# Small tiles moved to one constant tile, the global tokens' block moved to last but one, and the last store cut in parts

## The chip, the cores and the metric

The kernel runs on one core of a Trainium2 chip, in one launch. The metric is device time in microseconds (us), lower is better. Matrix products run on the tensor engine (PE, with PEld for the loads of its stationary operand). The vector engine (DVE), the scalar engine (ACT) and GpSimd (POOL) do the rest, and SyncE (SP) issues all DMAs, in one queue.

## What is computed

Eight batches of eight heads of attention with 32 global tokens and 512 local ones, and behind it a gated layer without a non-linearity:

```python
s_g = scale * q_g @ k_all.T          # 32 global queries see all 544 keys
s_l = scale * q_l @ [k_g, k_l].T     # 512 local queries: the global keys, and local ones within 32 positions
out_g, out_l = sm(s_g) @ v_all, sm(s_l) @ v_all
x = concat(out_g, out_l)             # (8 * 544, 512): all heads of a token side by side
a, b = x @ w1, x @ w2                # 512 -> 1024
return ((a * b) @ w3) @ w_out        # 1024 -> 1024 -> 512
```

## The kernel before, in words

Precision: a matrix product of two float32 operands is made of three products of the fast type fp32r. Each operand is split in a high part (a copy rounded to fp32r, `hi_of`) and a low part (what is left, `lo_of`), and high by high, low by high and high by low are summed in PSUM.

Attention: for each head `scores` (L528; L521 for the first 16 heads) makes the band of local scores in four windows, `minus_max` (L532, DVE) adds the mask and finds the maxima (tile `mn`, four numbers a row), `exps` (L536, ACT) makes the exponentials and their sums (`sm`), transposes (L565) turn them, and `values` (L641, L646) multiplies by v. The global queries of two heads go together: `g_scores` (L696, L688), maxima `mg`, sums `smg`. Tile `G` of `values` takes some of its columns through DRAM: `move_out` writes `gd`, `move_in` (L598) reads it back, both by SP's queue.

The layer: w3 and w_out are folded into one matrix at the start (`fold`, L934; result `w34`, high and low part). The tokens then pass in 17 blocks: 16 of 256 local tokens (two to a batch) and one of the 256 global tokens of all batches. A block has four quarters. In a quarter `first` makes two 128-row tiles of a and two of b: for each, over four pairs of heads p, three matmuls of 256 columns,

```python
nc.tensor.matmul(d, wh[:, k, c, :], x[:, 0, 0:w], ...)   # L797
nc.tensor.matmul(d, wh[:, k, c, :], x[:, 1, 0:w], ...)   # L798
nc.tensor.matmul(d, wl[:, k, c, :], x[:, 0, 0:w], ...)   # L799
```

so that a part of w1 and w2 (tiles `w12h`, `w12l`) is the stationary operand and the tokens (`x`) are the moving one. `gate_a` (ACT) and `gate_b` (DVE) multiply a by b, `gh` and `gl` are the two parts of that product, and `second` (L827 to L829) multiplies it by w34: the stationary operand is 128 columns of `gh` or `gl`, the moving one 512 columns of `w34`. After the fourth quarter `evict` (L834) copies the two accumulators of a block to SBUF (`o`) and `store` (L842; L844 for the global block) writes them to DRAM. Block 16, the last, is the global one (`quarter`: `key, w = (divmod(k, 2), 256) if k < 2 * B else ((B, 0), TG)`).

Order: every step is put on a list with the engines that may run it, an assumed duration, what it waits for, and a due time out of the table `DUE`. `list_schedule` plays the engines forward with the assumed durations and gives the free engine the ready step that is due first. The outcome is the order in each engine's queue. At run time every engine takes its queue strictly in that order.

Memory: tiles of a pool lie one behind the other in SBUF in the order in which their tags first appear, each rounded up to a multiple of 32 bytes. The pools follow each other: `const`, `p1`, `p2`, `w12a`, and then `early` and in its place `w12b`.

Of the kernel before, what the change touches and what calls it, by code (L numbers as in the profile page):

```python
# [30 lines left out]
def i(ap):  # L31
# [285 lines left out]
def band_attention_glu_kernel(  # L317
# [527 lines left out]

    def unpack(step, raw, dst):
# [606 lines left out]
```

## Time and profile before

| | |
|---|---|
| time, median of 3 runs | 877.1 us (876.62 to 877.37) |
| the profiled execution | 877.64 us, of which the span from first to last instruction is 875.9 us |
| TensorE clock granted | 0.995 of full speed over the span |
| PE busy | 849.7 us (97%) |
| DVE, ACT, POOL busy | 561.0, 538.3, 404.5 us |
| DMA | 109.75 MB, 125 GB/s mean |

The span is what the profile shows engine by engine, and the time has 1.7 us more around it. Matmuls are pipelined: the duration that the profile gives for one is longer than the distance from its start to the next one's start, and it is that distance, called pitch here, that adds up to the span.

### The profile page before, as it was taken

To read this page: it belongs to the slowest core of one execution; us is meant where nothing else is said; L and a number is where in the kernel's file an instruction comes from. 1 tells how busy PE (TensorE), PEld (TensorE's weight loads), DVE (VectorE), ACT (ScalarE), POOL (GpSimd) and SP (SyncE) were. 2 spreads that over 40 slices of the span, in tenths; PEclk is the share of its full clock that TensorE was granted. 3 is DMA by queue.
4 is the path that set the end of the run, shared out by engine and by line. 5 is a ranking of instruction groups with operands and counts; after the bars stand their busy time and mean duration, and the time that the engine had idled before them with its cause. 6 is when DMAs were issued, how large, how long until landed. Compare 5 with 4: busy or idle time off the path is not lost.

```text
span 875.9 us, 17696 instructions
## 1 busy us (share of the span) xinstructions
PE 849.7 (97%) x5794; PEld 766.2 (87%) x5794; DVE 561.0 (64%) x1464; ACT 538.3 (61%) x1450; POOL 404.5 (46%) x505
## 2 busy tenths in 40 slices
PE   4999999999999999999999999999999999999995
PEld 3666579899999999999999999999999999999994
DVE  3778777756777776779677777676757677421111
ACT  3666777756677777767676767776857677312111
POOL 1022445654665556656465656566666545200000
PEclk9999999999999999999999999999999999999998
DMA  8686655554746464655455645655555534100000
GB/s 280 201 264 219 198 158 139 159 118 93 160 94 171 100 149 97 146 132 147 100 132 130 155 105 124 144 128 135 127 137 123 128 95 96 27 25 1 25 25 25
DMA packets 194228, 109.75 MB, mean 125 GB/s; under 512 B 150040, under 2 KB 158232, under 8 KB 194136
## 3 DMA queue, kind: packets, MB, share of 16 engines
q1 hardware_dynamic: 194136, 108.61, 48.5%
q8 instruction: 46, 0.75, 0.4%
q14 instruction: 46, 0.38, 0.2%
HBM read 85.52 MB, written 20.28 MB: 121 GB/s over the span
## 4 chain that ended last, share of the span: by engine, by line
PE 92%; DMA 2%; POOL 1%; issue 1%; SPq 1%; DVE 1%; ACT 1%; POOLq 0%; DVEq 0%; ACTq 0%
PE bp L797 7%; PE ap L797 7%; PE bp L798 7%; PE bp L799 7%; PE ap L799 7%; PE ap L798 7%; PE acc L827 7%; PE acc L829 7%; PE acc L828 7%; PE av L646 7%; PE w L934 6%; PE s L528 5%; PE s L521 3%; PE t L565 3%; PE av L641 3%; PE sg L696 1%
## 5 line engine op out<-in xcount | busy, mean ns | idle before, releaser
L797 PE MATMUL ap<-x,w12h 128*128 128x256 f32 x544 | 156.6, 288 | 0.0
L797 PE MATMUL bp<-x,w12h 128*128 128x256 f32 x544 | 156.1, 287 | 0.0
L799 PE MATMUL ap<-x,w12l 128*128 128x256 f32 x544 | 154.3, 284 | 0.0
L798 PE MATMUL ap<-x,w12h 128*128 128x256 f32 x544 | 154.2, 283 | 0.0
L798 PE MATMUL bp<-x,w12h 128*128 128x256 f32 x544 | 154.1, 283 | 0.0
L799 PE MATMUL bp<-x,w12l 128*128 128x256 f32 x544 | 154.0, 283 | 0.0
L536 ACT ACTIVATE P<-P,mn 128x192 f32<-128x192 f32 (+1 forms) x256 | 121.3, 475 | 16.9 <-DVE mn L532 16.7
L797 PEld LDWEIGHTS ap<-x,w12h 128*128 128x128 f32 x544 | 104.0, 191 | 2.2 <-issue 0.4
L798 PEld LDWEIGHTS ap<-x,w12h 128*128 128x128 f32 x544 | 104.3, 192 | 1.6
L797 PEld LDWEIGHTS bp<-x,w12h 128*128 128x128 f32 x544 | 104.1, 191 | 1.7 <-issue 0.2
L798 PEld LDWEIGHTS bp<-x,w12h 128*128 128x128 f32 x544 | 104.2, 191 | 1.5
L799 PEld LDWEIGHTS ap<-x,w12l 128*128 128x128 f32 x544 | 104.2, 192 | 0.0
L799 PEld LDWEIGHTS bp<-x,w12l 128*128 128x128 f32 x544 | 104.1, 191 | 0.0
L532 DVE CUSTOM_DVE_ANT_0 P<-s,cs 128x192 f32<-128x192 f32 (+1 forms) x256 | 87.0, 385 | 26.4 <-PE s L528 18.0
L452 POOL TENSOR_TENSOR kl<-kr,kh 128x608 fp32r<-128x608 f32 x42 | 63.7, 1516 | 38.3 <-ACT kh L449 30.6
L660 DVE TENSOR_TENSOR u<-av,cb 64x352 f32<-64x352 f32 x112 | 57.5, 518 | 36.6 <-ACT cb L449 34.9
L449 ACT COPY cb<-av 64x352 f32<-64x352 f32 x94 | 41.9, 446 | 40.1 <-PE av L646 38.7
L646 PE MATMUL av<-PT,vs 128*128 128x192 f32 x448 | 64.4, 271 | 0.0
L646 PEld LDWEIGHTS av<-PT,vs 128*128 128x128 f32 x448 | 60.2, 190 | 0.8
L934 PE MATMUL w<-wo,w3f 128*128 128x512 f32 x128 | 60.1, 605 | 0.0
L452 POOL TENSOR_TENSOR TT<-TT 128x352 fp32r<-128x352 f32 x35 | 34.8, 993 | 44.9 <-ACT TT L449 39.8
L452 POOL TENSOR_TENSOR qs<-qr,qs 64x512 fp32r<-64x512 f32 x34 | 45.1, 1326 | 20.9 <-ACT qs L449 15.8
(807 smaller groups left out, 2148.7 us busy)
## 6 DMA issues: line engine op xcount, KB each, us to landing
kr<-in_kd_t_dram SPq DMA_DIRECT2D x96, 152.0 KB, 3.0
raw_w<-in_w_t_dram SPq DMA_DIRECT2D x24, 512.0 KB, 4.9
kpr<-in_kp_t_dram SPq DMA_DIRECT2D x32, 272.0 KB, 3.4
out_dram<-o SPq DMA_DIRECT2D x34, 256.0 KB, 2.9
R<-rd SPq DMA_DIRECT2D x64, 128.0 KB, 3.2
gd<-TT SPq DMA_DIRECT2D x112, 64.0 KB, 2.6
vr<-in_v_t_dram SPq DMA_DIRECT2D x28, 256.0 KB, 3.0
G<-gd SPq DMA_DIRECT2D x112, 64.0 KB, 2.7
```

Of the source, the lines that this page charges most:

```text
L452: (eng or nc.gpsimd).tensor_sub(dst, src, f(hi))
L532: nc.vector.tensor_tensor_reduce(blk(n, e), T["st", n][:, e, 0 : WIN[e][1]], masks[e], -0.125, 3.0e38, ALU.add, ALU.min, T["mn", n][:, e : ...
L536: nc.scalar.activation(blk(n, e), blk(n, e), AF.Exp, bias=T["mn", n][:, e : e + 1], scale=-1.0, accum_out=T["sm", n // 2][:, n % 2, e : e ...
L646: nc.tensor.matmul(av[:, o : o + 32 * (s1 - s0)], v, PT[:, s0:s1, y, j], start=False, stop=(j % 2 == 1 and (plain or y == 1)), skip_group_ ...
L660: nc.vector.tensor_add(T["u", n // 2][r : r + 64, x], T.pop(("av", n, x))[r : r + 64, 0:352], T["cb", n][r : r + 64, x])
L797: nc.tensor.matmul(d, wh[:, k, c, :], x[:, 0, 0:w], start=(k == m % 2 == 0), stop=False, skip_group_check=True)
L798: nc.tensor.matmul(d, wh[:, k, c, :], x[:, 1, 0:w], start=False, stop=False, skip_group_check=True)
L799: nc.tensor.matmul(d, wl[:, k, c, :], x[:, 0, 0:w], start=False, stop=(k == 3), skip_group_check=True)
L827: nc.tensor.matmul(a, gh[:, m % 2, sl], wh, start=(m == 0), stop=False)
L828: nc.tensor.matmul(a, gh[:, m % 2, sl], wl, start=False, stop=False)
L829: nc.tensor.matmul(a, gl[:, m % 2, sl], wh, start=False, stop=(m == 7))
L934: nc.tensor.matmul(T["w34", t], T["w3f", t, j // 4][:, j % 4], T["wo"][:, j], start=(j == 0), stop=(j == 7))
```

## The change

A tile `small` of 64 bytes is allocated in `const`, and `mn`, `mg` and `smg`, until now tiles of 32 bytes each in `p2` (two of `mn`) and `p1`, become slices of it. It stands in front of `w34`, whose tiles are allocated later. So the start of many tiles shifts by 64 bytes. In the built programs they begin at these addresses modulo 128:

| tiles | used as | before | now |
|---|---|---|---|
| w12h, w12l | stationary in `first` | 64 | 0 |
| x | moving in `first` | 64 | 64 |
| gh, gl | stationary in `second` | 64 | 64 |
| w34 | moving in `second` | 0 | 64 |
| QG | stationary in `g_scores` | 0 | 64 |
| kph, kpl (and their second halves) | moving in `g_scores` | 64 (0) | 64 (0) |
| vgs | stationary, L641 | 0 | 0 |
| vs | stationary, L646 | 64 | 64 |
| G, PT | moving, L641 and L646 | 0 | 64 |
| qs; kh, kl | stationary; moving in L528 | 64; 64 | 64; 64 |

The global block becomes block 15 and the second half of the last batch block 16. In the last quarter of block 16 the second product of one 128-token tile is made in two halves of 256 columns, each copied and stored by itself. The other tile stays whole. The numbers of `DUE` are all replaced, with a few more of them, since there are more steps. The code lines are one to three lower or higher in the new program (L797 is L798 there, L827 is L830, L834 is L837, L842 is L845).

```diff
 DUE = tuple(int(x) / 100 for x in """
-    -655 -3767 4986 -976 9590 1663 3525 1681 -604 7022 298 5732 -137 5816 154 5532 -86 5558 180 5514 -1205 5768 -3363 1416
+    1514 -13720 -3729 -9726 1511 -1470 2180 -5679 -837 8859 -6169 8856 2561 8285 -7174 8072 2818 8049 7770 7400 -1214 8643 6068 3083
...
+    small = const.tile([128, 16], F32, tag="small", name="small")
...
-        T["mn", n] = p2.tile([128, 4], F32, tag="mn", name=f"mn{n}")
+        T["mn", n] = small[:, 4 * (n % 2) : 4 * (n % 2) + 4]
...
-            T["mg", m // 2] = p1.tile([128, 1], F32, tag="mg", name=f"mg{m}")
+            T["mg", m // 2] = small[:, 8:9]
...
-        T["smg", g] = p1.tile([128, 1], F32, tag="smg", name=f"smg{g}")
+        T["smg", g] = small[:, 9:10]
...
-        for t in range(0, w, 128) if ts is None else ts:
+        c = slice(0, 512) if ts is None or len(ts) == 1 else slice(256 * ts[1], 256 * ts[1] + 256)
+        for t in range(0, w, 128) if ts is None else ts[:1]:
...
-        key, w = (divmod(k, 2), 256) if k < 2 * B else ((B, 0), TG)
+        key, w = (((B, 0), TG) if k == 2 * B - 1 else (divmod(min(k, 2 * B - 1), 2), 256))
...
-        split = k % 2 == 0 and q == 0
+        split = key[1] == 0 and q == 0
...
-        parts = [(e,) for e in range(0, w, 128)] if last else [None]
+        parts = [(0,), (128, 0), (128, 1)] if last else [None]
...
+            for e, h in [(0, None), (128, 0), (128, 1)] if last else [(e, None) for e in range(0, w, 128)]:
...
-        add(("xh", B, p, 0), only("ACT", COST["xh"]), base(NH) + 34, g, split_x, (B, p, 0), 0, xg[:, p], TG, 0)
-        add(("xl", B, p, 0), either("xl"), base(NH) + 35, [("xh", B, p, 0)],
+        add(("xh", B, p, 0), only("ACT", COST["xh"]), base(NH) + 8, g, split_x, (B, p, 0), 0, xg[:, p], TG, 0)
+        add(("xl", B, p, 0), either("xl"), base(NH) + 9, [("xh", B, p, 0)],
```

The built order shows the shift at three places. First SP's queue at the start of the program, before: `kq` holds the keys and `qp` the queries of the first two heads, `kpr` the keys for the global queries, `cs` identity and mask, `raw_w`, `raw_w12s` and `raw_wo` weights.

```order
L394 DMA qp_97<-in_q_t_dram 128x512
L424 DMA kpr_99<-in_kp_t_dram 128x544
L430 DMA QG_95<-in_qg_t_dram 64x4x32 x2
L370 DMA cs<-in_cst_dram 128x576
L898 DMA raw_w12s_0_108<-in_w_t_dram 128x512
L898 DMA raw_w_0_110<-in_w_t_dram 128x1024
L898 DMA raw_w12s_1_114<-in_w_t_dram 128x512
L400 DMA kq_116<-in_kd_t_dram 128x608
L424 DMA kpr_118<-in_kp_t_dram 128x544
L898 DMA raw_wo_0_120<-in_wo_t_dram 128x1024
```

The same place now:

```order
L425 DMA kpr_98<-in_kp_t_dram 128x544
L896 DMA raw_w_0_100<-in_w_t_dram 128x1024
L431 DMA QG_96<-in_qg_t_dram 64x4x32 x2
L401 DMA kq_106<-in_kd_t_dram 128x608
L395 DMA qp_110<-in_q_t_dram 128x512
L371 DMA cs<-in_cst_dram 128x576
L896 DMA raw_w12s_1_113<-in_w_t_dram 128x512
L896 DMA raw_w12s_0_117<-in_w_t_dram 128x512
L896 DMA raw_w12s_2_119<-in_w_t_dram 128x512
L425 DMA kpr_121<-in_kp_t_dram 128x544
L896 DMA raw_wo_0_123<-in_wo_t_dram 128x1024
```

`kq` has moved from eighth place to fourth (QG's row counts once), in front of `cs` and of all of `raw_w12s`. The weights `raw_w` have moved up to second place, in front of QG.

Second the end of PE's queue, before: the last quarter of the global block, `second` for its last two rows of `w34`.

```order
L827 MATMUL acc_0_128_11066<-w34h_937,gh__11188 128x512
L828 MATMUL acc_0_128_11066<-w34l_938,gh__11188 128x512
L829 MATMUL acc_0_128_11066<-w34h_937,gl__11196 128x512
L827 MATMUL acc_0_0_11065<-w34h_937,gh__11188 128x512
L828 MATMUL acc_0_0_11065<-w34l_938,gh__11188 128x512
L829 MATMUL acc_0_0_11065<-w34h_937,gl__11196 128x512
L827 MATMUL acc_0_0_11065<-w34h_1000,gh__11188 128x512
L828 MATMUL acc_0_0_11065<-w34l_1001,gh__11188 128x512
L829 MATMUL acc_0_0_11065<-w34h_1000,gl__11196 128x512
L827 MATMUL acc_0_128_11066<-w34h_1000,gh__11188 128x512
L828 MATMUL acc_0_128_11066<-w34l_1001,gh__11188 128x512
L829 MATMUL acc_0_128_11066<-w34h_1000,gl__11196 128x512
```

The same place now, the second half of the last batch. Ahead of these rows stand six more of 256 columns like the first six.

```order
L830 MATMUL acc_1_128_10971<-w34h_935,gh__11093 128x256
L831 MATMUL acc_1_128_10971<-w34l_936,gh__11093 128x256
L832 MATMUL acc_1_128_10971<-w34h_935,gl__11101 128x256
L830 MATMUL acc_1_128_10971<-w34h_963,gh__11093 128x256
L831 MATMUL acc_1_128_10971<-w34l_964,gh__11093 128x256
L832 MATMUL acc_1_128_10971<-w34h_963,gl__11101 128x256
L830 MATMUL acc_1_0_10970<-w34h_935,gh__11093 128x512
L831 MATMUL acc_1_0_10970<-w34l_936,gh__11093 128x512
L832 MATMUL acc_1_0_10970<-w34h_935,gl__11101 128x512
L830 MATMUL acc_1_0_10970<-w34h_963,gh__11093 128x512
L831 MATMUL acc_1_0_10970<-w34l_964,gh__11093 128x512
L832 MATMUL acc_1_0_10970<-w34h_963,gl__11101 128x512
```

The tile that is cut in halves is finished first, and the whole tile, 512 columns wide, ends the queue.

Third the last rows of SP's queue, before: four stores of local tokens and the two of the global block.

```order
L842 DMA out_dram<-o_0_128_10753 128x512
L842 DMA out_dram<-o_0_0_10755 128x512
L842 DMA out_dram<-o_1_0_11041 128x512
L842 DMA out_dram<-o_1_128_11043 128x512
L844 DMA out_dram<-o_0_0_11210 4x32x512
L844 DMA out_dram<-o_0_128_11212 4x32x512
```

The same place now:

```order
L845 DMA out_dram<-o_0_0_None 128x512
L845 DMA out_dram<-o_0_128_None 128x512
L847 DMA out_dram<-o_0_0_None 4x32x512
L847 DMA out_dram<-o_0_128_None 4x32x512
L845 DMA out_dram<-o_1_128_0_11112 128x256
L845 DMA out_dram<-o_1_128_1_11121 128x256
L845 DMA out_dram<-o_1_0_None 128x512
```

The two global stores (4x32x512) stand one block earlier, and the queue ends with two half stores and a whole one of local tokens.

## Rows read from the trace of the kernel before

**Rows 1.** The page: span, and busy time of each engine.

```profile
span 875.9 us, 17696 instructions
PE 849.7 (97%) x5794; PEld 766.2 (87%) x5794; DVE 561.0 (64%) x1464; ACT 538.3 (61%) x1450; POOL 404.5 (46%) x505
```

**Rows 2.** Waits of PE over the span: for what, total us, times, longest.

```profile
PE sg L688 <- DMA QG<-in_qg_t_dram: 5.2, 1, 5.2
PE s L521 <- DMA kq<-in_kd_t_dram: 4.9, 1, 4.9
PE av L641 <- DMA G<-gd: 2.2, 2, 1.2
PE s L521 <- DVE mg L715: 1.2, 1, 1.2
```

**Rows 3.** Timeline of PE in block 16: start us, duration us, instruction.

```profile
857.45 0.28 PE L797 MATMUL bp<-x,w12h 128*128 128x256 f32 x1
...
860.20 0.28 PE L799 MATMUL bp<-x,w12l 128*128 128x256 f32 x1
860.32 0.40 PE L827 MATMUL acc<-w34h,gh__11164 128*128 128x512 f32 x1
...
863.12 0.39 PE L827 MATMUL acc<-w34h,gh__11188 128*128 128x512 f32 x1
```

**Rows 4.** Windows: busy us of each engine, then PEclk, DMA share, GB/s.

```profile
800.00:840.00 40.00, 40.00 (x285) 37.50 (x284) 6.92 (x10) 6.49 (x11) 0.00 (x0) 1.00 0.04 15
840.00:866.00 26.00, 26.00 (x167) 23.24 (x165) 5.44 (x8) 4.76 (x8) 0.00 (x0) 1.00 0.06 21
```

**Rows 5.** The page's groups: line, operation, count | busy us, mean ns.

```profile
L797 PE MATMUL ap<-x,w12h 128*128 128x256 f32 x544 | 156.6, 288 | 0.0
L799 PE MATMUL bp<-x,w12l 128*128 128x256 f32 x544 | 154.0, 283 | 0.0
```

**Rows 6.** Timeline of SP at the end: start us, us, engine, operation.

```profile
865.42 1.29 ACT L834 COPY o<-acc 128x512 f32<-128x512 f32 x2 [3.56 <-PE acc L829]
865.69 0.40 PE L829 MATMUL acc<-w34h,gl__11196 128*128 128x512 f32 x1
866.03 1.40 SPq L844 DMA_DIRECT2D out_dram<-o  x2
```

**Rows 7.** Waits of SP's queue, 860 to 877 us: for what, us, times, longest.

```profile
SPq L1454 <- DMA out_dram<-o: 7.4, 1, 7.4
```

**Rows 8.** Windows in the last store and in a local block's stores, columns as above.

```profile
870.00:872.00 2.00, 0.00 (x0) 0.00 (x0) 0.00 (x0) 0.00 (x0) 0.00 (x0) 0.63 0.26 101
810.80:811.80 1.00, 1.00 (x11) 1.00 (x10) 0.95 (x2) 0.00 (x0) 0.00 (x0) 1.00 1.01 385
```

**Rows 9.** DMA issues, 809 to 816 us: count, KB each, median us to landing.

```profile
out_dram<-o SPq DMA_DIRECT2D x2, 256.0 KB, 2.1
```

**Rows 10.** The chain that ended last, in the first 25 us: start, us, what.

```profile
5.09 6.97 DMA kq<-in_kd_t_dram
12.06 0.14 issue
12.20 3.33 PE s L521 x8
...
16.94 2.18 PE sg L688 x4
19.12 1.66 PE w L934 x2
```

**Rows 11.** Windows at the start, columns as above.

```profile
3.00:12.10 9.10, 2.15 (x4) 1.18 (x4) 3.10 (x8) 1.56 (x3) 1.57 (x4) 1.00 0.92 290
25.00:30.00 5.00, 5.00 (x22) 3.64 (x21) 3.64 (x13) 3.11 (x12) 0.00 (x0) 1.00 0.62 179
```

**Rows 12.** L696's first kph matmul at 186 us: duration ns min/median/max.

```profile
L696 PE MATMUL sg<-kph,QG x1: 284/284/284, 186.0 to 186.0; 128*128 128x272 f32 x1
```

**Rows 13.** L696's next two matmuls, at 186.1 and 186.2 us.

```profile
L696 PE MATMUL sg<-kph,QG x1: 288/288/288, 186.1 to 186.1; 128*128 128x272 f32 x1
L696 PE MATMUL sg<-kpl,QG x1: 288/288/288, 186.2 to 186.2; 128*128 128x272 f32 x1
```

**Rows 14.** Groups of PE by form, 200 to 760 us: busy us, mean ns.

```profile
L641 PE MATMUL av<-G,vgs 128*128 128x256 f32 x50 | 14.4, 287 | 0.0
```

More of the change, by code (lines that the diff above doesn't have):

```diff
@@ L823, in second, with evict, store @@
         gh, gl = T["gh", m // 2 % 2], T["gl", m // 2 % 2]
-        for t in range(0, w, 128) if ts is None else ts:
+        c = slice(0, 512) if ts is None or len(ts) == 1 else slice(256 * ts[1], 256 * ts[1] + 256)
+        for t in range(0, w, 128) if ts is None else ts[:1]:
             sl = slice(t, t + tw)
-            a = T["acc", key, t][0:tw]
-            nc.tensor.matmul(a, gh[:, m % 2, sl], wh, start=(m == 0), stop=False)
-            nc.tensor.matmul(a, gh[:, m % 2, sl], wl, start=False, stop=False)
-            nc.tensor.matmul(a, gl[:, m % 2, sl], wh, start=False, stop=(m == 7))
-    def evict(key, w, t, eng=None):
-        tw = min(w, 128)
-        o = p2.tile([128, 512], F32, tag="o", name=f"o{key[0]}_{key[1]}_{t}", bufs=NO)
-        (nc.scalar.copy if eng is nc.scalar else nc.vector.tensor_copy)(o[0:tw], T.pop(("acc", key, t))[0:tw])
-        T["o", key, t] = o
-    def store(key, w, t):
-        tw = min(w, 128)
-        o = T.pop(("o", key, t))
+            a = T["acc", key, t][0:tw, c]
+            part = dict(skip_group_check=m > 5)
+            nc.tensor.matmul(a, gh[:, m % 2, sl], wh[:, c], start=(m == 0), stop=False, **part)
+            nc.tensor.matmul(a, gh[:, m % 2, sl], wl[:, c], start=False, stop=False, **part)
+            nc.tensor.matmul(a, gl[:, m % 2, sl], wh[:, c], start=False, stop=(m in (5, 7)), **part)
+    def evict(key, w, t, cols=None, eng=None):
+        tw, c = min(w, 128), slice(0, 512) if cols is None else slice(256 * cols, 256 * cols + 256)
+        o = p2.tile([128, 512], F32, tag="o", name=f"o{key[0]}_{key[1]}_{t}_{cols}", bufs=NO)
+        (nc.scalar.copy if eng is nc.scalar else nc.vector.tensor_copy)(o[0:tw, c], T["acc", key, t][0:tw, c])
+        T["o", key, t, cols] = o
+    def store(key, w, t, cols=None):
+        tw, c = min(w, 128), slice(0, 512) if cols is None else slice(256 * cols, 256 * cols + 256)
+        o = T.pop(("o", key, t, cols))
         if key[0] < B:
             r = key[0] * S + 32 + 256 * key[1] + t
-            nc.sync.dma_start(out[r : r + 128], o)
+            nc.sync.dma_start(out[r : r + 128, c], o[:, c])
         else:
@@ L1291, in quarter @@
                         take("acc", 2, ("acc", k, e), me)
-                add(me, only("PE", COST["second"] * c / len(parts)), u + 1.1 * j + (ts[0] / 64 if ts else 0), deps, second, key, w, m + j, ts)
+                add(me, only("PE", COST["second"] * c / (2 * len(ts) if ts else 1)), u + 1.1 * j + (sum(ts) / 64 if ts else 0), deps, second, key, w, m + j, ts)
                 read(me, ("gh", n), ("gl", n), *[("acc", k, e) for e in range(0, w, 128)])
         if q == 3:
-            for e in range(0, w, 128):
-                me = ("out", k, e)
-                take("o", NO, ("o", k, e), me)
-                add(me, dict(ACT=(COST["out"], False, 0), DVE=(691, False, HOLD_A)), u + 2.5, [("second", k, 7, (e,) if last else None)],
-                    evict, key, w, e, eng=True)
+            for e, h in [(0, None), (128, 0), (128, 1)] if last else [(e, None) for e in range(0, w, 128)]:
+                me = ("out", k, e, h)
+                take("o", NO, ("o", k, e, h), me)
+                ns = (COST["out"], 691) if h is None else (340, 420)
+                add(me, dict(ACT=(ns[0], False, 0), DVE=(ns[1], False, HOLD_A)), u + 2.5 + 0.5 * (h or 0),
+                    [("second", k, 7, (e,) if h is None else (e, h)) if last else ("second", k, 7, None)], evict, key, w, e, h, eng=True)
                 read(me, ("acc", k, e))
-                add(("store", k, e), dma(390), u + 3.0, [me], store, key, w, e, nbytes=262144)
-                read(("store", k, e), ("o", k, e))
+                add(("store", k, e, h), dma(390), u + 3.0 + 0.5 * (h or 0), [me], store, key, w, e, h, nbytes=262144 if h is None else 131072)
+                read(("store", k, e, h), ("o", k, e, h))
     def made(m):
```

330 rows, old and new, of the table DUE are left out of this document.

## The prediction

> **What bounds the kernel now.** I read the page first: PE is busy 849.7 of 875.9 us, the next engine 561.0 [rows 1]. Then PE's waits: 5.2 and 4.9 us for the first loads, and in the other 850 us three waits of together 3.4 [rows 2]. Nearly all the rest of PE's idle time lies behind its last matmul (865.69 plus 0.40 us) [rows 6]. So the span is a head in which PE waits for data, a body in which PE issues one matmul behind the other, and a tail. The body is the number of matmuls times their pitch, and the timeline gives that. In the last block 24 matmuls of `first` start between 857.45 and 860.32, a pitch of 2.87 / 24 = 119.6 ns, and 12 of `second` start between 860.32 and 863.12, a pitch of 233.3 ns [rows 3]. The granted clock there is 1.00, the level of 2.4 GHz, and the other engines and the DMAs hardly work [rows 4]. At one column per cycle 256 columns take 106.7 ns and 512 take 213.3. So 12.9 and 20.0 ns of each matmul are something else, in a stretch where nobody disturbs PE but PE itself. `first` has 6 lines of 544 [rows 5], 3264 matmuls, and `second` 17 blocks x 8 x 2 x 3 = 816: 390 and 190 us of the span.
>
> **Tail: the last store.** Before, the second copy out of PSUM ends at 865.42 + 1.29 = 866.71. Its store is issued until 866.03 + 1.40 = 867.43, and SP then waits 7.4 us, until 874.8, for it to land [rows 6, 7]. That is 8.1 us from the copy to the landing, with 1.1 us of closing rows behind it. The windows say why: the global store runs at a DMA share of 0.26 and 101 GB/s, a quarter of the engines, and the local stores of the same size, in a quiet stretch, at 1.01 and 385 GB/s [rows 8]. Those land 2.1 us after their issue [rows 9]. Now the last store is a local one of a whole tile, so copy to landing takes about 2.3 us: a gain of 5.8. The copy before it stays 0.6 us long, since the order ends with the whole tile, not with a half. The halves of the other tile have 6 x 233 ns = 1.4 us for their copies and issues, so they are out of the way. If their data still hold up the last store, the gain is 5.0; 6.0 is the other end. Halving makes six matmuls into twelve: 12 x 119.6 - 6 x 233.3 ns = 0.04 us. The global stores are now issued some 23 us before the end, with only the three last stores behind them in SP's queue: hidden. If the last block were shorter than 8 us they would be the end again.
>
> **Head.** PE's first long wait ends when `kq` lands, 6.97 us after its issue [rows 10]. In SP's order 2208 KB stand up to and with `kq` before (the sizes in the rows of the order, four bytes an element). Now 1408 KB stand up to and with `kq` and `qp`, 800 KB less. At the 290 GB/s of that stretch [rows 11] the first scores start 2.8 us earlier. Against that, QG comes behind 512 KB of weights, 256 KB net, 0.9 us later, still ahead of `kq`. `cs`, which the maxima need, comes behind both, but before the scores have ended. What is late next is the second `kpr` (264 KB of loads more ahead of it net, 0.9 us), and the folded weights, on which PE lives from 19 us on. PE is fully busy from 25 us [rows 11], so only what moves in the 25 us before counts. I take 1.5 us of 2.8, between all and nothing.
>
> **Body, the order.** All due numbers change, so the queues are shuffled everywhere. What a better order can win in the body are the three waits, 3.4 us [rows 2]; each new wait of that kind would cost 1.2. With no view that tells which, I take 0, and 2.5 us either way. The slices of `small` add no wait: each was a tile of its own before, with the same readers and writers, and the maxima's rows wait for the scores alone in both programs.
>
> **Body, the addresses.** This is the largest and least known term. `first` goes from stationary 64, moving 64 (modulo 128) to stationary 0, moving 64. One operation of the trace has that last state: `g_scores`, in its first half of `kph` and of `kpl`. Its second halves have both at 0, with the same stationary tile and 272 columns. The first `kph` half takes 284 ns, the second 288; the first `kpl` half takes 288, too [rows 12, 13]. So the new state is worth 4 ns or none. I take 2 ns: 3264 x 2 = 6.5 us. `second` goes the other way, from moving 0, stationary 64 to both at 64, and if equal starts are what costs, it loses the same 2 ns: 804 x 2 = 1.6 us. The rows leave more room. For `second` the lower end is a gain of 20.0 - 12.9 = 7.1 ns, 5.7 us, if a moving tile that starts at 64 is what makes `first` lose less than `second`. For `first` the upper end is a loss of 4 ns, 13.1 us: a matmul of 256 columns with both operands at 0 (L641) takes 287 ns [rows 14], and `first`, with both at 64, 283 [rows 5], so a stationary start at 0 may be the bad one. The attention's other matmuls (L646, L641, `g_scores`, some 670) change state in both directions. At 2 ns that is 1.3 us at most, and I take 0.
>
> The Trainium skill, page "SBUF — State Buffer", section "Who interferes with whom", says that TensorE reads its moving operand and its weights through two independent ports and never waits on anyone; by that the addresses would change nothing, and the sum below would be 6.5 - 1.6 = 4.9 us higher. The page "TensorE: Matmul & The Clock Gate", section "Back-to-back issue gap", gives N / 2.4 + 2.5 ns, which is 109.2 and 215.8 ns here; the trace disagrees with its 119.6 and 233.3 [rows 3], so some 10 and 17 ns are lost to what neither rule names.
>
> **Sum.** -5.8 (tail) - 1.5 (head) + 0 (order) - 6.5 (`first`) + 1.6 (`second`) = -12.2 us. The profiled execution took 877.64, 0.5 above the median; against the median, 877.1 - 12.2 = 864.9, said as **865**.
>
> **Rivals.**
> - *The addresses do nothing.* PE's loss comes from elsewhere, and the pitches stay at 119.6 and 233.3. For it: the first `kpl` half is no faster than the second, and the loss of `second`, 20.0 ns, is larger than that of `first` although its starts differ already. Then tail and head are left: 877.1 - 7.3 = 869.8.
> - *The addresses do more.* `first` gains the full 4 ns, 13.1 us, and `second` up to 5.7, since its moving tile now starts at 64 like x. For it: the 7.1 ns between the two losses, and the 4 ns of the `kph` pair. Against it: `kpl`. 877.1 - 7.3 - 13.1 - 5.7 = 851 to 856.7 with `second` unchanged; said as 853.
> - *The addresses do harm, and the kernel is slower.* A stationary start at 0 costs `first` 4 ns, as the 287 against 283 ns can be read: 877.1 - 7.3 + 13.1 = 882.9. It decides from 7.3 / 3264 = 2.2 ns on. Against it: the neighbours of L641 are strided matmuls, those of `first` are not, and the `kph` half that is fast has its stationary operand at 0.
>
> New waits of the shuffled order would shift each case by about 1.2 us a piece; six of them would be needed to cancel tail and head.
>
> **How the numbers follow.** Forecast (the addresses give a part, 858 to 869): 0.45. They do nothing: 0.29. They do more: 0.17. They do harm: 0.09. The range of 8 in 10 leaves out the harm and some of the far ends: 853 to 873. A measurement here tells 0.2% (1.75 us) from no change. The first three cases are all faster than that, except where new waits eat the 7.3 us of the second: faster 0.89, within 0.2% 0.03, slower 0.08.
>
> **What would show it.** Tail: SP's last wait falls from 7.4 to about 1.7 us, and from the last matmul to the end of the span there are some 4 us instead of 9.8. Head: the first L522 matmul starts at 9.4 us instead of 12.2, and PE is fully busy some 1.5 us earlier. Addresses: the mean duration of L798 to L800 falls from 283 to about 281 ns, and 24 of them take 2.82 us instead of 2.87. `second` rises to 235 ns. The prediction is wrong if the pitch of `first` stays, falls by more than 4 ns or rises, or if PE's waits in the body grow beyond the 3.4 us of before.

## The result, and the profile after

The changed kernel takes 862.87 us (median of 4 runs, 861.14 to 864.45), the kernel before, beside it, 876.86 (4 runs, 876.18 to 877.37): a ratio of 0.984, 95% interval 0.9815 to 0.9866. The prediction was 865.0, 853 to 873. The profiled execution took 861.5 us, with a span of 859.7. First its page, with the two groups that answer to [rows 1, 5].

```profile
span 859.7 us, 17696 instructions
PE 841.6 (98%) x5800; PEld 758.7 (88%) x5800; DVE 564.2 (66%) x1481; ACT 533.6 (62%) x1439; POOL 400.5 (47%) x500
L798 PE MATMUL ap<-x,w12h 128*128 128x256 f32 x544 | 154.0, 283 | 0.0
L800 PE MATMUL bp<-x,w12l 128*128 128x256 f32 x544 | 151.9, 279 | 0.0
```

The mean of `first` has fallen from 288 to 283 ns and from 283 to 279. Next the timeline of PE in the last block, as in [rows 3].

```profile
846.51 0.28 PE L798 MATMUL bp<-x,w12h 128*128 128x256 f32 x1
...
849.34 0.40 PE L830 MATMUL acc<-w34h,gh__11069 128*128 128x512 f32 x1
...
852.07 0.28 PE L830 MATMUL acc<-w34h,gh__11093 128*128 128x256 f32 x1
...
853.02 0.28 PE L832 MATMUL acc<-w34h,gl__11101 128*128 128x256 f32 x1
853.76 0.39 PE L830 MATMUL acc<-w34h,gh__11093 128*128 128x256 f32 x1 [0.46 <-ACT o L837]
...
855.38 0.39 PE L832 MATMUL acc<-w34h,gl__11101 128*128 128x512 f32 x1
```

24 products of `first` take 2.83 us where they took 2.87, and 12 of `second` 2.73 where they took 2.80. So both products have become shorter. Over all products that stand between two of their own kind (2918 and 592 in the changed kernel; the mean distance from start to start, without the distances that hold a wait), `first` goes from 119.4 to 117.5 ns and `second` from 233.4 to 230.1. A wait is new: the second half of the cut tile begins 0.74 us after the product before it, where 0.12 is usual.

The tail, in the timeline of ACT and SP, as in [rows 6]:

```profile
855.81 0.58 ACT L837 COPY o_None<-acc 128x512 f32<-128x512 f32 x1 [1.01 <-PE acc L832]
856.42 0.33 SPq L845 DMA_DIRECT2D out_dram<-o_None  x1
```

and in the waits of SP's queue, as in [rows 7]:

```profile
SPq L1453 <- DMA out_dram<-o_None: 1.7, 1, 1.7
```

From the start of the last matmul to the end of the span it is 859.7 - 855.38 = 4.3 us, and was 875.9 - 865.69 = 10.2. The head, in the chain that ended last, as in [rows 10]:

```profile
4.13 4.86 DMA cs<-in_cst_dram
...
9.12 0.72 DVE Pg L716
...
9.90 3.36 PE s L522 x8
...
14.68 2.18 PE sg L689 x4
...
23.39 1.71 PE s L522 x8
25.10 0.68 PE av L642 x2
```

with the rows of the kernel before that answer to the last two,

```profile
24.24 1.75 PE s L521 x8
25.99 0.68 PE av L641 x2
```

and in PE's waits of the first 25 us, as in [rows 2]:

```profile
PE sg L689 <- DMA QG<-in_qg_t_dram: 6.5, 1, 6.5
PE sg L689 <- DVE small L533: 1.4, 1, 1.4
PE s L522 <- DVE small L716: 1.2, 1, 1.2
PE tg L735 <- DVE Pg L729: 0.8, 1, 0.8
```

The first L522 starts at 9.90 us instead of 12.20, but no longer waits for `kq`: it waits for the maxima of the global scores (L716), which hold its PSUM tile, and these wait for `cs`, which has moved behind `kq` and `qp`. The first L689 starts 1.3 us later than before, since QG stands behind `raw_w`. Of the 2.3 us 2.26 are still there when L689 comes the second time (14.68 us instead of 16.94). Where L642 begins, 40 matmuls of the same kinds lie behind PE in both kernels, and the lead is 25.99 - 25.10 = 0.9 us; it is still 0.9 at 80 us. The rest was lost in between, where PE waits for DVE (0.8 us for `Pg`, 0.3 for `w3f`). So the head gained 0.9 us. (The expectations of two experiments below reckon with a loss of 14.8 us in both kernels, and so with no gain; the starts of the same matmuls show the gain.) In both kernels the first scores also run at half the pace of later ones: eight take 3.36 us at 9.90 and 1.71 at 23.39. The windows give a granted clock of 1.00 in the head, too [rows 11], which doesn't fit these durations.

One thing in the profile of before is not in the rows above. Its windows at 160 to 166 us (columns as in [rows 4]):

```profile
160.00:162.00 2.00, 0.84 (x7) 0.60 (x7) 1.48 (x4) 1.69 (x4) 0.20 (x2) 1.00 0.45 114
...
164.00:166.00 2.00, 2.00 (x12) 2.00 (x11) 1.93 (x9) 1.56 (x5) 2.00 (x2) 0.50 0.51 140
```

Behind PE's wait of 1.16 us for L715 the granted clock fell to 0.50, the level of 1.2 GHz, and 16 products of `first` took 3.4 us instead of 1.9. In the profiled execution of the changed kernel PE has the same wait (1.1 us, from 159.4 on), and the clock stays at 1.00.

The difference of the spans, 16.2 us, is thus: tail 5.9; `first` 3264 x 1.9 ns = 6.2; `second` 804 x 3.3 ns = 2.7; the clock 1.5; head 0.9; the halves -0.6; and -0.4 of small things.

### The profile page after: what moved, and what is told of

Read it like the earlier page. It is cut to its first block, busy times and chain, and to the rows that moved or that the text cites. A ratio compares the mean times of both kernels' runs of the same rounds, so it can differ in the third digit from the quotient of the medians.

```text
span 859.7 us, 17696 instructions
## 1 busy us (share of the span) xinstructions
PE 841.6 (98%) x5800; PEld 758.7 (88%) x5800; DVE 564.2 (66%) x1481; ACT 533.6 (62%) x1439; POOL 400.5 (47%) x500
## 4 chain that ended last, share of the span: by engine, by line
PE 87%; DMA 5%; issue 2%; POOL 2%; DVE 2%; SPq 1%; ACT 1%; DVEq 0%; POOLq 0%; ACTq 0%
PE bp L798 7%; PE bp L800 7%; PE bp L799 7%; PE ap L798 7%; PE ap L800 7%; PE ap L799 7%; PE acc L830 7%; PE acc L832 7%; PE acc L831 7%; PE av L647 6%; PE s L529 5%; PE w L932 4%; PE t L566 3%; PE s L522 2%; PE av L642 2%
## 5 line engine op out<-in xcount | busy, mean ns | idle before, releaser
L798 PE MATMUL bp<-x,w12h 128*128 128x256 f32 x544 | 154.2, 283 | 0.0
L798 PE MATMUL ap<-x,w12h 128*128 128x256 f32 x544 | 154.0, 283 | 0.2 <-ACT as__7961 L804 0.2
L800 PE MATMUL ap<-x,w12l 128*128 128x256 f32 x544 | 152.0, 279 | 0.0
L799 PE MATMUL ap<-x,w12h 128*128 128x256 f32 x544 | 151.9, 279 | 0.0
L799 PE MATMUL bp<-x,w12h 128*128 128x256 f32 x544 | 151.8, 279 | 0.0
L537 ACT ACTIVATE P<-P,small 128x256 f32<-128x256 f32 (+1 forms) x256 | 121.4, 476 | 18.8 <-DVE small L533 18.1
L798 PEld LDWEIGHTS ap<-x,w12h 128*128 128x128 f32 x544 | 102.2, 188 | 2.0 <-ACT as__7961 L804 0.6
L798 PEld LDWEIGHTS bp<-x,w12h 128*128 128x128 f32 x544 | 102.2, 188 | 1.7 <-issue 0.6
L799 PEld LDWEIGHTS ap<-x,w12h 128*128 128x128 f32 x544 | 102.4, 188 | 1.2
L799 PEld LDWEIGHTS bp<-x,w12h 128*128 128x128 f32 x544 | 102.3, 188 | 1.1
L453 POOL TENSOR_TENSOR kl<-kr,kh 128x608 fp32r<-128x608 f32 x36 | 55.0, 1526 | 35.6 <-ACT kh L450 30.7
L450 ACT COPY cb<-av 64x352 f32<-64x352 f32 x87 | 38.8, 446 | 30.1 <-PE av L647 28.8
L453 POOL TENSOR_TENSOR vs<-vr,vs 128x256 fp32r<-128x256 f32 x42 | 33.2, 794 | 51.7 <-ACT vs L450 39.3
L453 POOL TENSOR_TENSOR qs<-qr,qs 64x512 fp32r<-64x512 f32 x37 | 48.1, 1299 | 19.7 <-ACT qs L450 10.5
```

The source lines that it names most:

```text
L453: (eng or nc.gpsimd).tensor_sub(dst, src, f(hi))
L537: nc.scalar.activation(blk(n, e), blk(n, e), AF.Exp, bias=T["mn", n][:, e : e + 1], scale=-1.0, accum_out=T["sm", n // 2][:, n % 2, e : e ...
L798: nc.tensor.matmul(d, wh[:, k, c, :], x[:, 0, 0:w], start=(k == m % 2 == 0), stop=False, skip_group_check=True)
L799: nc.tensor.matmul(d, wh[:, k, c, :], x[:, 1, 0:w], start=False, stop=False, skip_group_check=True)
L800: nc.tensor.matmul(d, wl[:, k, c, :], x[:, 0, 0:w], start=False, stop=(k == 3), skip_group_check=True)
```

## The experiments

All but one are changes to the changed kernel, and differ from it by what the diff shows. The executions of one kernel lie 1 to 6 us apart in most of them, in two 8 and 11, so the pitch, read from the trace, tells more of the addresses than the time.

**Which starts count: the change of addresses undone, and each half of it.**

```diff
# small_undone: the four lines with small as before (tiles mn in p2, mg and smg in p1)
# first_only
-    small = const.tile([128, 16], F32, tag="small", name="small")
+            if m == 0: T["small"] = p1.tile([128, 16], F32, tag="small", name="small")
# second_only
+        if n == 0: nc.vector.memset(p2.tile([128, 16], F32, tag="pad", name="pad", bufs=1), 0.0)
```

> The changed kernel with `small` taken out again: mn, mg and smg are tiles in p2 and p1 as before, and all starts are those of before (w12 64, x 64, gh 64, w34 0, modulo 128). Order, blocks and last store stay those of the changed kernel. Theory (the starts set the pitch): `first` goes back from 117.6 to 119.4 ns (5.9 us) and `second` from 231 to 234.5 ns (2.9 us); about 871 us against the 861 to 864 of the changed kernel. Rival (the new order, not the starts, shortened the pitches): both pitches stay, 861 to 865 us.

> The changed kernel with `small` as a tile of p1: w12 begins at 0 as now, but w34 at 0 as before (x and gh 64; QG, PT and G as before). Theory (starts, and each of the two products by its own operands): `first` stays at 117.6 ns, `second` goes back to 234.5; 865 us, 3 more than the changed kernel. Rival (one cause for both, for instance w12's place alone or the order): both pitches stay as in the changed kernel, 861 to 864 us.

> The changed kernel with 64 more bytes in p2 ahead of w12: w12 begins at 64 as before, w34 at 64 as now. Theory: `first` goes back to 119.4 ns, `second` keeps 231; 868 us, 6 more than the changed kernel. Rival (order): both pitches stay, 861 to 864 us.

Then three kernels with other pairs of starts.

```diff
# x0_w0
-            T["sm", n // 2] = p2.tile([128, 2, 4], F32, tag="sm", name=f"sm{n}", bufs=2)
+            if n == 0: T["sms"] = p1.tile([128, 2, 2, 4], F32, tag="sms", name="sms")
+            T["sm", n // 2] = T["sms"][:, n // 2 % 2]
# x0_w64
+        if n == 0: nc.vector.memset(p1.tile([128, 16], F32, tag="pad", name="pad"), 0.0)
# x96_w32
+        if n == 0: nc.vector.memset(p1.tile([128, 8], F32, tag="pad", name="pad"), 0.0)
```

> The changed kernel with the sums sm (64 bytes) moved from p2 to p1, ahead of x: x and gh begin at 0, w12 at 0, w34 at 64. It asks what about the starts matters. If it is the stationary operand's own start, `first` stays at 117.6 ns and `second` gains too (stationary at 0 now, 229 ns): 860 us. If it is that the two starts differ, `first` (0, 0) goes back to 119.4 or worse and `second` (64, 0) gains: 866 us. If a moving operand at 64 is what is good, `first` loses 2 ns (6 us) and `second` stays: 868 us.

> The changed kernel with 64 more bytes in p1, ahead of x: x and gh begin at 0, w12 at 64, w34 at 64 (modulo 128). Theory for `first` (what counts is that the two starts lie 64 bytes apart): 117.5 ns, as in the changed kernel. Rival (the moving operand has to begin at 64, the stationary one at 0): both are wrong here, 119 ns or more. `second` has the pair of the run with x and w12 at 0 (64, 0) and stays at 233.2 ns by either. Time: 864.5 us by the theory, 869 by the rival.

> The changed kernel with 32 more bytes in p1, ahead of x: x and gh begin at 96, w12 at 32, w34 at 64. `first` again has 64 bytes between its starts, at other starts; `second` has 32 bytes (64, 96). If only the distance counts, `first` stays at 117.5 ns; if the starts themselves do, it goes to 119 or more (5 us). `second` lies between its 230 ns of equal starts and its 233.3 of 64 bytes apart; 231.7 in the middle. Time: 863 to 866 us if the distance counts, 867 to 871 if not.

Measured, with the starts modulo 128 of the moving and the stationary operand, the mean pitch over all products, and the time of 24 `first` and 12 `second` in the last block, read from the timeline as above:

| kernel | `first`: starts | pitch ns | 24 take us | `second`: starts | pitch ns | 12 take us | median us | ratio to before (95%) |
|---|---|---|---|---|---|---|---|---|
| before | 64, 64 | 119.4 | 2.87 | 0, 64 | 233.4 | 2.80 | | |
| small_undone | 64, 64 | 119.4 | 2.87 | 0, 64 | 233.5 | 2.81 | 870.77 | 0.9915 (0.9890 to 0.9940) |
| first_only | 64, 0 | 117.6 | 2.82 | 0, 64 | 233.3 | 2.81 | 866.74 | 0.9881 (0.9846 to 0.9917) |
| second_only | 64, 64 | 119.5 | 2.87 | 64, 64 | 230.4 | 2.75 | 868.69 | 0.9888 (0.9858 to 0.9918) |
| changed | 64, 0 | 117.5 | 2.83 | 64, 64 | 230.1 | 2.73 | 862.87 | 0.984 (0.9815 to 0.9866) |
| x0_w0 | 0, 0 | 119.0 | 2.88 | 64, 0 | 233.2 | 2.80 | 869.34 | 0.9899 (0.9869 to 0.9929) |
| x0_w64 | 0, 64 | 117.6 | 2.83 | 64, 0 | 233.2 | 2.80 | 867.10 | 0.9876 (0.9847 to 0.9905) |
| x96_w32 | 96, 32 | 117.7 | 2.82 | 64, 96 | 232.5 | 2.80 | 865.73 | 0.9864 (0.9848 to 0.9880) |

The rows of two of them, PE in the last block of x0_w0:

```profile
854.12 0.28 PE L800 MATMUL bp<-x,w12h 128*128 128x256 f32 x1
...
857.00 0.40 PE L832 MATMUL acc<-w34h,gh__11038 128*128 128x512 f32 x1
...
859.80 0.28 PE L832 MATMUL acc<-w34h,gh__11062 128*128 128x256 f32 x1
```

and of x0_w64:

```profile
850.86 0.28 PE L800 MATMUL bp<-x,w12h 128*128 128x256 f32 x1
...
853.69 0.39 PE L832 MATMUL acc<-w34h,gh__11071 128*128 128x512 f32 x1
...
856.49 0.28 PE L832 MATMUL acc<-w34h,gh__11095 128*128 128x256 f32 x1
```

The first three were expected at 871, 865 and 868 us, and took 870.8, 866.7 and 868.7. x0_w0 is none of its three cases as a whole: `first` went back, as in the second, but `second` did not gain. x0_w64 took 867.1, between the 864.5 and 869 of its two cases, with executions 5.7 us apart, so there the pitch decides. The order of the steps is the same in the seven kernels from small_undone on, so the pitches follow the starts: the order rival falls. The two products change apart from each other, each with its own operands. For `first` the distance of its two starts counts, not the starts: 64 bytes apart gives 117.5 to 117.7 in three places, equal starts give 119.0 and 119.4. So x0_w64 fits the theory of the distance, and the rival, for which both operands were in the wrong place, falls. For `second` it is the other way round: equal starts (measured at 64, 64 alone) give 230, 64 bytes apart 233.2 to 233.5, and 32 apart 232.5, nearer to the bad end than to the middle.

Is it the number of columns that turns the rule round, or something else about `second`? The halved tile of the last block settles it, since there the same operands are read 256 columns at a time. In the changed kernel, with equal starts, nine of these matmuls start between 852.07 and 853.02 (above), 118.8 ns apart. In first_only, with starts 64 apart, it is

```profile
856.57 0.28 PE L831 MATMUL acc<-w34h,gh__11093 128*128 128x256 f32 x1
...
857.48 0.28 PE L833 MATMUL acc<-w34h,gl__11101 128*128 128x256 f32 x1
```

or 113.8 ns, while the 512 columns of the same kernel take 233.3. The other kernels agree: 0.95 us for the eight distances with equal starts (second_only), 0.91 or 0.92 with 64 apart (small_undone, x0_w0, x0_w64), 0.94 with 32 apart. So 256 columns want the two starts 64 bytes apart and 512 want them equal, at the very same addresses. Nothing here shows why. Nor is the period of 128 bytes tested by itself: modulo 512, too, the moving operand of `first` starts 64 bytes above the stationary one in all kernels with the short pitch, and only the equal starts were seen at two distances, 0 (119.4 and 119.5 ns) and 128 (119.0, x0_w0).

**The tail: the kernel before, with its last stores in another form.**

```diff
-            nc.sync.dma_start(out.rearrange("(b s) c -> b s c", s=S)[t // 32 : (t + tw) // 32, 0:32], o[0:tw])
+            for j in range(4):
+                nc.sync.dma_start(out[(t // 32 + j) * S : (t // 32 + j) * S + 32], o[32 * j : 32 * j + 32])
```

> The kernel before with each of the two global stores issued as four, one for each batch's 32 rows (32x512 each instead of 4x32x512); nothing else changes. Theory (the last store is slow because of its form, whose outermost dimension is 4, and works a quarter of the DMA engines): each piece spreads over all engines, the last one lands some 2 us after its issue; with three more issues of 0.4 us ahead of it the end comes 4 to 5 us earlier, 872.5 us. Rival (the rows lie apart in DRAM, or the end of the program is slow for another reason): the DMA share stays at 0.26 and the time at 877, or 1 us more for the issues.

873.9 us (7 runs), 0.9953 of before (0.9938 to 0.9969), 3.4 us at the medians. Its timeline of SP:

```profile
864.55 3.64 SPq L845 DMA_DIRECT2D out_dram<-o  x8
```

A window after the last issue, columns as in [rows 4]:

```profile
868.20:869.30 1.10, 0.00 (x0) 0.00 (x0) 0.00 (x0) 0.00 (x0) 0.00 (x0) 0.50 0.45 119
```

SP's last wait is 1.1 us instead of 7.4 [rows 7], and the DMA share behind the last issue 0.45 instead of 0.26 [rows 8]. The rows lie as far apart in DRAM as before, so the form was the cause. The gain is less than the 4 to 5 us of the theory: from the last matmul's start to the end it is 6.2 us instead of 10.2, and 3.64 of them go into the eight issues. This run changes two things of the form, the outermost dimension and the number of pieces under way. The changed kernel parts them, since its last store is as large as one of the global ones and in one piece, with 128 rows outermost:

```profile
out_dram<-o_None SPq DMA_DIRECT2D x1, 256.0 KB, 2.0
```

It lands 2.0 us after its issue, and from the last start to the end it is 4.3 us. So it isn't the number of pieces.

**The halves.** The step of the first half makes all 512 columns, that of the second nothing.

```diff
-        c = slice(0, 512) if ts is None or len(ts) == 1 else slice(256 * ts[1], 256 * ts[1] + 256)
-        for t in range(0, w, 128) if ts is None else ts[:1]:
+        c = slice(0, 512)
+        for t in range(0, w, 128) if ts is None else ts[:1] * (1 not in ts):
```

> The changed kernel with the last block's second tile whole again: its last six products are 512 columns wide, then one copy and one store; the order stays. Theory (the halves cost more than 0.04 us, since the second half of a tile waits for the copy of its first half): PE's wait of 0.5 us for ACT o near 853 us is gone, and with it 0.7 us; 860.5 to 863.5 us. Rival (the halves hide their copies and issues behind PE's last products): the whole tile's copy and issue hold up the last copy and the last store, 0 to 0.6 us slower than the changed kernel.

862.66 us, 0.9853 (0.980 to 0.9907): no difference that the time shows. In the trace the wait for ACT o at the end is gone, SP's last wait is 1.7 us as in the changed kernel, and nothing takes its place there (4.1 us from the last start to the end). So the 0.6 to 0.7 us that the halves cost are seen in the place where they were lost, but not in the median: in this execution PE's waits for G<-gd alone are 2.5 us instead of 1.0, and the four executions lie 11 us apart.

**The head.** First the loads alone in the order of need, then also the steps that unpack them, together with the whole tile of the last experiment.

```diff
# loads_by_need
+        for key in [("load", "q2", 0), ("load", "k2", 0), ("load", "cs"), ("load", "qg", 0), ("load", "kp", 0), ("clear", "QG", 0)]:
+            queue.insert(0, queue.pop(at(key)))
# head_and_whole, first as above; w3, w12, loads: raw_w's and raw_w12s' early steps, raw_w12s' loads
+        for group, key in ((first, None), (w3, ("exps", 0, 3)), (w12, ("exps", 1, 3)), (loads, ("fetch", "wo", 0, 0))):
+            part = [queue.pop(at(k)) for k in group]
+            p = at(key) + 1 if key else 0
+            queue[p:p] = part
```

> The changed kernel with the first loads in SP's queue in another order: kpr, QG, cs, kq, qp, and then raw_w and the rest as it was. Theory (the head gained nothing because cs lands at 9.0 us, and the first maxima, and through their PSUM tile the first scores, wait for it): L522 starts by 8.3 us instead of 9.9, PE's idle time in the first 50 us (14.8 us in both kernels) falls by 1.5; about 861.4 us at the median. Rival (the head hangs on the weights and on DVE's queue): L522 starts earlier, but PE waits as much longer for w3f and the weights, which now come 3 us later; 862 to 865 us.

> The changed kernel with the second tile of the last block whole, and with the head put in order on all queues, not on SP's alone: loads kpr, QG, cs, kq, qp, raw_w, kpr, raw_wo, then raw_w12s; on DVE and ACT the unpacking of raw_w stands behind the maxima and exponentials of head 0, and that of raw_w12s behind those of head 1. Theory (the slower run with the loads alone in this order lost its time because DVE's queue began with raw_w, which then came 5 us later): the first L716 starts at 7 us instead of 9.1, L522 by 8 us, and PE is 1.5 to 2.5 us further on at 25 us; with the 0.7 us of the halves 859 to 861 us. Rival (what is moved back, raw_w and raw_w12s, is then missing for the folds): PE's idle time in the first 50 us stays at 14 us or more, and only the 0.7 us are left, 861 to 864.

loads_by_need took 866.46 us, 0.9875 (0.9852 to 0.9899), 3.6 more than the changed kernel. Its timeline at the start:

```profile
4.49 2.15 PE L689 MATMUL sg<-kpr,QG 128*128 128x272 f32 x4 [4.49 <-DMA QG<-in_qg_t_dram]
...
11.17 0.43 DVE L852 TENSOR_SCALAR raw_w<-raw_w 128x512 int32<-128x512 int32 x1 [11.17 <-DMA raw_w<-in_w_t_dram]
11.89 0.69 DVE L856 SCALAR_TENSOR_TENSOR w3f<-raw_w 128x512 int32<-128x512 int32 x1 [0.29 <-ACT raw_w L854]
12.50 0.71 DVE L716 CUSTOM_DVE_ANT_1 Pg<-sg,cs 64x544 f32<-64x544 f32 x1
...
13.27 2.28 PE L522 MATMUL s<-kq,qp 64*128 64x192 f32 x5 [6.63 <-DVE small L716]
```

Neither theory had this, though the rival named DVE's queue: L522 starts later, not earlier. QG came 2.0 us earlier, but DVE's queue begins with the unpacking of `raw_w`, whose load now stood behind the others; L716 stood behind that step with its data ready, and PE behind L716. With those steps moved too (head_and_whole) L716 started at 6.53 and L522 at 7.85, as expected, and the second head's scores at 21.99 instead of 23.32. Yet the time is 863.29 us, 0.983 (0.9813 to 0.9847), the same as the changed kernel's. The windows of that profile:

```profile
10.00:20.00 10.00, 6.78 (x23) 4.35 (x21) 7.14 (x21) 5.10 (x16) 0.00 (x0) 0.95 1.05 342
20.00:30.00 10.00, 9.08 (x35) 5.87 (x34) 7.09 (x24) 6.25 (x20) 0.00 (x0) 0.88 0.66 227
160.00:170.00 10.00, 9.66 (x54) 8.85 (x55) 8.24 (x33) 7.68 (x22) 6.91 (x8) 0.83 0.47 116
```

The same matmuls, side by side, show where the lead over the changed kernel went. It is 2.05 us at the first L522, 1.1 where L642 begins (23.91 instead of 25.03) and gone at the L936 of 29.90 us (29.94 in the changed kernel). The first half of it went between 20 and 24 us, where the granted clock was low in this profile and not in the changed kernel's. The second half went into a wait of 0.9 us ahead of that L936, for `wo`, the weights that DVE unpacks for the fold. An earlier wait for them stands in the timeline:

```profile
16.74 1.13 PE L936 MATMUL w<-wo,w3f 128*128 128x512 f32 x2 [0.71 <-DVE wo L860]
```

That is the rival: what was moved back is missing for the folds. At 160 us the lower clock cost another 10 x 0.17 = 1.7 us. Whether the order of the loads made the clock fall isn't shown.

**The wait at 160 us.** Two ways to fill it: 12 products of `first` ahead of the scores of head 12, or the six of `second` that stood ahead of `g_scores` (this one with the last tile whole).

```diff
# scores_later; moved: ("s", 12) and the steps up to y = b that depend on it
+        queue[a : b + 1] = [queue[y] for y in stay + moved]
# wait_filled; y: the last "second" step ahead of a = ("s", 12)
+        queue.insert(a - 1, queue.pop(y))
```

> The changed kernel with one step of PE moved: the scores of head 12 stand behind the next 12 products of `first`, so that they don't wait for the maxima of L716 at 159 us. Theory (the wait of 1.1 us is PE's own loss, and the lower granted clock that followed it in the profiled execution of before also explains the two groups of times of the changed kernel, 861 and 864): the wait is gone, and all executions lie at 860 to 861 us, with a mean granted clock of 1.00. Rival (the two groups have another cause): the wait goes, 1.1 us less in both groups, 860 and 863 us. Second rival: the maxima come as much later and the wait shows up at the next step; no gain.

> The changed kernel with the second tile of the last block whole, and with one step of PE moved at 157 us: the last six products of `second` stand between the transposes of head 11 and the scores of head 12, instead of ahead of g_scores, so that the maxima of L716 are made meanwhile. Theory (that wait of 1.1 us is pure loss, and the lower granted clock behind it, which the profiles of some kernels show at 160 to 170 us and others don't, is what parts the executions of the changed kernel into 861 and 864): the wait is gone, the granted clock stays at 1.00 there, and the executions come together at 859.5 to 861.5 us. Rival (the wait only moves: the last part of w12 for block 0 is late instead, as when the scores were moved behind `first`): 862 to 865 us, with a wait of L798 for ACT w12h.

scores_later took 867.27 us, 0.988 (0.9852 to 0.9908). PE's waits at 150 to 180 us:

```profile
PE bp L798 <- ACT w12h L450: 1.7, 1, 1.7
PE bp L800 <- POOL w12l L453: 0.3, 1, 0.3
```

The products pulled ahead met the last piece of `w12h`, which wasn't made yet: the wait moved to the next step and grew, as in the second rival, though for `w12h` and not for the maxima, and the granted clock at 160 to 170 us was 0.74. wait_filled left 0.4 us of the 1.1, with no wait for w12h and the clock at 1.00 there, but took 863.24 us (860.18 to 868.38), 0.9822 (0.9799 to 0.9845). Its profiled execution was the longest of the five, and its windows show where:

```profile
20.00:30.00 10.00, 9.06 (x22) 5.86 (x23) 5.19 (x16) 3.60 (x12) 0.00 (x0) 0.59 0.62 193
...
130.00:140.00 10.00, 8.76 (x55) 8.24 (x54) 5.81 (x19) 6.26 (x18) 5.27 (x8) 0.83 0.71 196
```

So the clock can fall at other places too, and the wait at 160 us isn't what parts the executions. Nor does the mean clock alone: two of its executions have spans of 858.3 at 0.999 and 861.4 at 1.000. What makes the 3 us between executions stays open. Of the seven kernels in one order, which all have that wait, one profile (x0_w0) shows the clock low there, 0.83 over 160 to 170 us, and the other six show 1.00. No kernel here is measurably faster than the changed one.

## Why the prediction was right, and where not

- **Tail, -5.8.** It measured -5.9, by the step as put, and the form of the last store as its cause is shown (0.26 of the DMA engines' time with 4 rows outermost; a store as large with 128 lands in 2.0 us). The Trainium skill, page "DMA: Bandwidth & Descriptors", section "Why a DMA increments its semaphore by 16 and not by 1", says that a transfer is dealt to the largest number of engines up to 16 that divides the outermost dimension of both sides: 4 for 4x32x512, 16 for 32x512. The trace agrees: a share of 0.26, about 4 of 16 engines, there [rows 8], and more, 0.45, with the pieces.
- **`first`, -6.5.** 1.9 ns instead of 2, 6.2 us. The reason that was given, equal starts cost, is what the runs show for this product. The size is luck: it is the middle of "4 ns or none", and the 4 ns of [rows 12] needn't come from the addresses (below).
- **`second`, +1.6.** Here the step failed: "if equal starts are what costs, it loses the same 2 ns". `second` gains 3.3 ns from equal starts, 2.7 us. What holds for 256 columns was carried over to 512 without a row, and the same operands at 256 columns do lose by equal starts (118.8 ns instead of 113.8). The other end (7.1 ns, from the smaller loss of `first`) had the right sign.
- **Head, -1.5.** It measured -0.9, between all and nothing as put, but for other reasons. The first scores started 2.3 us earlier, not 2.8, since behind `kq` there was at once `cs`, and behind `cs` the maxima on DVE. Then 1.4 us of the 2.3 were lost again by 25 us, where PE waits for DVE. (The loads more ahead of the second `kpr` are 256 KB by the order, not 264; the 0.9 us hold.)
- **Order, 0.** PE's waits between 25 and 840 us were 3.4 us [rows 2] and are 3.6.
- **Halves, +0.04.** 0.6 us. The count of matmuls was right, but the second half writes into the tile whose first half ACT copies, and waits for that copy. A wait that the change adds was overlooked.

The row that the price of `first` was taken from doesn't part the addresses from the order. Over 500 to 760 us of the kernel before, all with the same starts, the `kph` matmuls take (ns, min/median/max)

```profile
L696 PE MATMUL sg<-kph,QG x20: 283/287/312, 511.3 to 708.8; 128*128 128x272 f32 x20
```

and the first of each four takes 283 to 284 behind `first` at most places, 287 behind `second` (at 342.6 us) and 311 behind L646 (at 252.5 us). So what stands before it moves it by more than the 4 ns.

The errors are 4.3 us too little gain in `second`, against 0.6 each too much in the head and the halves, and -0.1 and +0.3 in tail and `first`: 864.9 - 4.3 + 0.6 + 0.6 - 0.1 + 0.3 = 862.0. The median is 862.87, and its four executions lie 3.3 us apart. That the forecast was only 2 us off is in part luck, as errors of both signs stand in it. The lower clock at 164 us in the profile of before is in none of these terms; the four executions of before agree within 1.2 us, so what it is worth at the median isn't known.

The rivals: that the addresses do nothing, or harm, is refuted by the pitches. That they do more was half right: `second` gained, as it said, but 2.7 of its 5.7 us, and `first` not the 4 ns. The page "SBUF — State Buffer" of the Trainium skill, section "Who interferes with whom", gives TensorE two independent read ports and says that it never waits on anyone. The prediction took that to mean that addresses change nothing, and the pitches disagree: 119.4 or 117.5 ns by nothing but the starts. Whether what is lost is a wait for a read, no run shows.

## What to carry to other kernels

Where one matmul follows the other, try the start addresses of its two operands against each other, for each shape by itself: 64 bytes more ahead of a tile were worth 1.6% of `first` and 1.4% of `second`, in opposite directions, and only the duration of the matmuls and the distance of their starts show it. End a program with a store whose outermost dimension fills the DMA engines: a last store with 128 rows outermost instead of 4 was worth 5.9 us here. Cutting the copy of a last tile in parts that share one PSUM tile cost 0.6 us, because the second part waited for the copy of the first; two tiles of their own were not tried. A load that is moved up helps only as far as the queues of the engines that unpack it are in the same order: the head of DVE's in-order queue held up PE for 6.6 us here.

## What the hardware showed that was not expected

- The pitch of these fp32r matmuls depends on the distance of the two operands' starts modulo 128, and the number of columns decides which way: in `first` (256 columns) 117.5 ns when they are 64 apart and 119.0 to 119.5 when equal, in `second` (512) 230 when equal and 233.3 when 64 apart, and with the operands of `second` at 256 columns 113.8 when 64 apart and 118.8 when equal. The better pitches of `first` and `second` are still 10.8 and 16.8 ns above the 106.7 and 213.3 that the prediction took as its measure.
- The granted clock fell to the 1.2 GHz level in the middle of the kernel, after PE had waited for 1.2 us and worked again for 2 us, which cost 1.5 us over 16 matmuls; after the same wait it didn't in the execution of another kernel. In others it was low at 20 to 30, 130 to 140 or 160 to 170 us.
